# Attention, then two feed-forward layers, on one core: another order of the nine steps of a head pair

## The chip, the cores and the metric

The kernel runs on one core of a Trainium2 chip. The metric is the device time of one execution in microseconds (us); lower is better. Before the change it is 1013.62 us, the median of 3 runs (1011.56 to 1013.67).

## What is computed

Attention with a learned position bias, then two feed-forward layers over the 4 x 576 tokens, all in float32:

```python
scores = scale * q @ k.transpose(0, 1, 3, 2)      # (4, 8, 576, 64) each
bias = np.maximum((psi_rel / psi_i)[..., None] @ w1 + b1, 0.0) @ w2
scores = scores + bias.transpose(2, 0, 1)[None]
attn = np.exp(scores - scores.max(-1)); attn = attn / (attn.sum(-1) + 1e-9)
x = attn @ v                                      # to (2304, 512)
h = x @ w_in                                      # (2304, 1024)
solu = h * softmax(h); ln = (solu - mean) / sqrt(var + 1e-6) * g_ln
x = ln @ w_out
g = clipped square of x @ moe2_w_in               # (2304, 2048)
return g @ moe2_w_out
```

## The kernel before, in words

The program has four stages: the bias tables; attention; the first feed-forward layer, pipelined over tiles of 128 tokens; the second one. Each operand of a score or feed-forward product is held as a rounded part and a remainder (kh and kl for k, both in one tile sq for q, wih and wil for the weights), so that products of the rounded type keep the accuracy. Making these pairs is work for VectorE (the cast) and GpSimd (the subtraction).

Attention is one loop over k (L586), 144 steps of scores and eight more to empty the pipeline. Sixteen units u (a pair of heads hp and a batch b) have nine steps n each: two heads times four tiles of 128 queries, and a ninth step that takes the last 64 queries of both heads. The instructions go to each engine's queue in the order in which the program emits them, and an engine takes its queue in order. That order is written out by hand: `order[n]` (L582) is a string of letters for step n, and each letter emits one piece of work:

- Q, `emit_qk` (L381): four score matmuls (eight in step 8; L394) into one of two score buffers ps_s in PSUM, then the eviction L400 on VectorE, which adds the bias tile bt and keeps the smallest of each row. A score buffer is free again when its eviction is done. In the last batch of a head pair, Q also issues the bias loads of the next pair on the SP queue (L202).
- E, `emit_exp` (L411): the exponential of that step on ScalarE (L415); it needs the eviction of its step.
- T, `emit_T` (L446): on TensorE the transposes (L457, four of them, and L464, L465 or L471 in some steps) of the exponentials of five steps before, into one of three buffers ps_t, and copies to pt: ScalarE (L458, L466, L472), and in step 4 two small ones on VectorE (L467, L468).
- P, `emit_pv` (L474): the products with v, seven steps behind. It emits something in steps 1, 5 and 6 alone: called PV0, PV1 and PV2 here (L486, L490). PV1 ends in a copy by ScalarE (L496), PV2 in one by VectorE (L498). PV0 and PV1 share the only buffer ps_x; PV2 takes one of ps_t.
- r, R, M, S, N, `emit_norm` (L422), for the unit before: r the reciprocals of the row sums (L426, L427, VectorE), R their transposes to a ps_t buffer (L433, TensorE), M the product of output and reciprocals (L435, VectorE), S one transpose more (L438, TensorE), N the last two products (L443, VectorE).
- B, one step of `prep_all` (L172) for the next unit's q and k. Four steps make one of the two heads: the cast kh (L181, VectorE); the subtraction kl (L183, GpSimd) and the cast sq (L184, VectorE); the subtraction into the lower half of sq (L186, GpSimd) with the next load of q and k on the SP queue (L162); nothing. Eight steps of B a unit make both heads, kh0 to sq0 and kh1 to sq1 in the texts below. B starts in unit 1 and has nothing left in unit 15.
- W, one step of `split_w` (L273), which decodes a piece of the float64 weights of the first feed-forward layer into the pair. Four phases make one piece: (1) the subtraction of the piece before (L281, GpSimd) and three integer and float operations on VectorE (L291, L294, L295); (2) a ScalarE operation (L299); (3) one VectorE operation (L301), a product on GpSimd (L304) and the load of the piece after next on the SP queue (L323, L327); (4) a scaling (L309, for half of the pieces) and a cast (L310), both on ScalarE. There are 32 pieces; W acts from k = 6 on. Nine W a unit and four phases a piece: the phases that fall to a place in the unit move on by one from unit to unit, and come round after four.

After the loop's 144 steps `tail` (L585) gives the letters of the last steps, and what is left of W is emitted at once (L591).

Of the kernel before, what the change touches and what calls it, by code (L numbers as in the profile page):

```python
# [35 lines left out]
def tile_attention_moe_moe(  # L36
# [504 lines left out]
    def emit_post(i):  # L541
# [38 lines left out]


    order = [  # L582
        "PQTWBE", "QBrWTPEW", "QTBWPBE", "QTPEBW", "QBPTEW", "QPTWRE", "QPBMWTSBE", "PQTNE", "QTPWE",
    ]
    tail = {1: "TPr", 5: "TPR", 6: "TPMS", 7: "TPN"}  # L585
    for k in range(NK + LP + 1):  # L586
# [356 lines left out]
```

## Time and profile before

| what | value |
|---|---|
| median of 3 runs | 1013.62 us |
| the profiled execution: its own time | 1013.55 us |
| the profiled execution: span, first to last instruction | 1011.8 us |
| granted TensorE clock, mean | 0.997 |
| TensorE busy | 971.6 us (96%) |
| VectorE busy | 654.8 us (65%) |
| ScalarE busy | 549.1 us (54%) |
| GpSimd busy | 310.6 us (31%) |

How to read it: these are shares of the whole span, and the four stages have different limits; the change acts only on the attention loop, whose units 1 to 14 lie between 85.6 and 355.0 us. PE is TensorE, DVE VectorE, ACT ScalarE and POOL GpSimd. A matmul's end is modelled and matmuls overlap, so TensorE's busy time also holds part of what it loses; the starts of its groups tell more. In the rows, "idle before <- releaser" is the idle time of the engine just ahead of the instruction and what ended it.

### The profile page before, as it was taken

How to read it: one execution, taken by the hardware profiler on the slowest of the kernel's cores; microseconds unless marked ns; L12 is line 12 of the kernel's file. 1: busy time of each engine (PE TensorE's matmuls, PEld its weight loads, DVE VectorE, ACT ScalarE, POOL GpSimd, SP SyncE). 2: the span in 40 equal slices, each digit the busy share in tenths (PEclk: the TensorE clock that was granted, in tenths of full speed). 3: DMA queues.
4: the chain of work that ended last, by engine and by line, in shares of the span. 5: the costliest groups of instructions: out<-in, count | busy, mean ns of one | idle time of the engine just before them, and what ended most of it. 6: DMA issues, size and time to landing. Idle time of an engine off the chain costs nothing.

```text
span 1011.8 us, 16200 instructions
## 1 busy us (share of the span) xinstructions
PE 971.6 (96%) x6112; PEld 801.4 (79%) x6112; DVE 654.8 (65%) x1232; ACT 549.1 (54%) x1116; POOL 310.6 (31%) x277
## 2 busy tenths in 40 slices
PE   9998998998998999999999999989999999999998
PEld 6447777777786787898988898768888888888897
DVE  6878898898888844777777755775434433343343
ACT  6887777777788775656566643343222223222232
POOL 3313455455455412344556442340010011000000
PEclk9999999999999999999999999999999999999999
DMA  6994363363364200024454458710100100000010
GB/s 190 286 298 141 135 207 118 136 205 121 126 203 129 67 22 22 33 84 146 147 177 157 147 200 306 270 66 1 63 22 1 62 11 11 21 32 11 1 42 21
DMA packets 50046, 112.21 MB, mean 111 GB/s; under 512 B 7600, under 2 KB 13872, under 8 KB 49968
## 3 DMA queue, kind: packets, MB, share of 16 engines
q1 hardware_dynamic: 42688, 101.72, 30.3%
q0 software_dynamic: 2384, 4.74, 1.8%
q10 hardware_dynamic: 4896, 4.72, 1.4%
q8 instruction: 48, 0.79, 0.3%
q14 instruction: 30, 0.25, 0.1%
HBM read 80.34 MB, written 30.82 MB: 110 GB/s over the span
## 4 chain that ended last, share of the span: by engine, by line
PE 39%; issue 7%; POOL 6%; DVE 5%; ACT 2%; DMA 1%; ACTq 0%; POOLq 0%; DVEq 0%
PE acc L844 17%; PE h L820 16%; PE ps_x L696 3%; PE ps_s L535 2%; POOL wp L304 2%; POOL wdl L281 2%; DVE ga L827 1%; POOL xl L519 1%; DVE wp L291 1%; DVE raw L294 1%; POOL stb L568 1%; DVE ga L828 1%; PE ps_s L696 1%; DVE wp L295 1%; DVE stb L570 1%
## 5 line engine op out<-in xcount | busy, mean ns | idle before, releaser
L827 DVE SCALAR_TENSOR_TENSOR ga<-ga 128x512 f32<-128x512 f32 (+1 forms) x80 | 56.8, 710 | 157.3 <-ACT ga L826 157.3
L400 DVE CUSTOM_DVE_ANT_0 e<-ps_s,bt 128x576 f32<-128x576 f32 x144 | 107.5, 754 | 34.6 <-PE ps_s L394 30.0
L826 ACT ACTIVATE ga<-h,half_c 128x512 f32<-128x512 f32 (+1 forms) x80 | 51.6, 645 | 130.9 <-PE h L820 130.9
L304 POOL TENSOR_TENSOR wp<-raw,wp 128x256 f32<-128x256 f32 (+1 forms) x64 | 67.3, 1051 | 176.0 <-DVE wp L301 149.0
L394 PE MATMUL ps_s<-kh,sq 128*128 128x288 f32 x320 | 103.4, 340 | 18.6 <-DVE su L400 18.6
L415 ACT ACTIVATE e<-e,su 128x576 f32<-128x576 f32 x144 | 112.9, 784 | 13.5 <-DVE su L400 13.5
L820 PE MATMUL h<-x2h,w2l 128*128 128x512 f32 (+1 forms) x320 | 117.7, 368 | 0.0
L820 PE MATMUL h<-x2l,w2h 128*128 128x512 f32 (+1 forms) x320 | 117.7, 368 | 0.0
L820 PE MATMUL h<-x2h,w2h 128*128 128x512 f32 (+1 forms) x320 | 117.6, 368 | 0.0
L844 PE MATMUL acc<-w2h,gh 128*128 128x512 f32 x288 | 112.7, 391 | 2.5 <-ACT gh L829 2.5
L844 PE MATMUL acc<-w2h,gl 128*128 128x512 f32 x288 | 112.5, 391 | 1.5 <-DVE gl L831 1.5
L844 PE MATMUL acc<-w2l,gh 128*128 128x512 f32 x288 | 112.3, 390 | 0.0
L829 ACT CAST gh<-ga 128x512 fp32r<-128x512 f32 (+1 forms) x80 | 46.4, 581 | 120.6 <-DVE ga L828 120.6
L733 POOL TENSOR_TENSOR x2l<-x2f,x2h 128x512 fp32r<-128x512 f32 (+1 forms) x20 | 25.7, 1287 | 253.5 <-ACT x2h L732 253.5
L458 ACT COPY pt<-ps_t 128x512 f32<-128x512 f32 x144 | 83.5, 580 | 21.5 <-PE ps_t L457 19.4
L394 PE MATMUL ps_s<-kl,sq 128*128 128x288 f32 x320 | 89.7, 296 | 0.0
L457 PE MATMUL ps_t<-ident,e 128*128 128x128 f32 x576 | 86.4, 273 | 1.0 <-ACT pt L458 0.9
L831 DVE TENSOR_TENSOR gl<-ga,gh 128x512 fp32r<-128x512 f32 (+1 forms) x80 | 52.2, 653 | 48.5 <-ACT gh L829 48.3
L394 PEld LDWEIGHTS ps_s<-kh,sq 128*128 128x128 f32 x320 | 61.4, 192 | 23.8 <-DVE su L400 22.0
L696 PE MATMUL ps_x<-lh,woh 128*128 128x256 f32 x256 | 74.2, 290 | 5.6 <-ACT os L701 5.6
L696 PE MATMUL ps_x<-ll,woh 128*128 128x256 f32 x256 | 72.7, 284 | 0.4 <-DVE ll L685 0.4
L457 PEld LDWEIGHTS ps_t<-ident,e 128*128 128x128 f32 x576 | 70.4, 142 | 3.4 <-ACT pt L458 1.6
(147 smaller groups left out, 2332.0 us busy)
## 6 DMA issues: line engine op xcount, KB each, us to landing
stg<-in_qk_dram SPq DMA_DIRECT2D x30, 640.0 KB, 4.2
raw<-in_w2nd_dram SPq DMA_DIRECT2D x32, 512.0 KB, 3.7
bias_d<-ow SPq DMA_DIRECT2D x36, 295.5 KB, 4.6
w_d<-wdh SPq DMA_DIRECT2D x20, 256.0 KB, 2.8
w_d<-wdl SPq DMA_DIRECT2D x20, 256.0 KB, 2.5
w2h<-w_d SPq DMA_DIRECT2D x10, 512.0 KB, 5.3
w2l<-w_d SPq DMA_DIRECT2D x10, 512.0 KB, 6.0
v<-in_vp_dram SPq DMA_DIRECT2D x15, 320.0 KB, 3.0
```

The costliest lines, as they stand in the source:

```text
L304: nc.gpsimd.tensor_tensor(out=p, in0=t, in1=p, op=ALU.mult)
L394: nc.tensor.matmul(sc[:, hf, 0:HS], lhsT=l, rhs=r, start=j == 0, stop=j == len(parts) - 1)
L400: nc.vector.tensor_tensor_reduce(out=halves(e), in0=sc[:, :, 0:HS], in1=halves(b_t[hp, n]), scale=-1.0 / float(D) ** 0.5, scalar=3.0e38, o ...
L415: nc.scalar.activation(out=e, in_=e, func=ACTF.Exp, scale=-1.0, bias=su[:, n:n + 1], accum_out=su[:, 9 + n:10 + n])
L457: nc.tensor.transpose(tp[:, kt * 128:(kt + 1) * 128], e[:, c0:c0 + 128], ident)
L458: nc.scalar.copy(out=pt[:, 4 * h:4 * h + 4, 128 * o:128 * o + 128], in_=tp.rearrange("p (a b) -> p a b", a=4))
L696: nc.tensor.matmul(ob[:, a * 256:(a + 1) * 256], lhsT=l, rhs=r[:, f, :], start=f == 0 and j == 0, stop=f == K1 - 1 and j == 2,)
L820: nc.tensor.matmul(hp_, lhsT=l, rhs=r[:, kk, 0:n], start=kk == 0 and q == 0, stop=kk == KD - 1 and q == 2)
L826: nc.scalar.activation(out=a, in_=hp_, func=ACTF.Relu, scale=0.5, bias=half_c)
L827: nc.vector.scalar_tensor_tensor(out=a, in0=a, scalar=1.0, in1=a, op0=ALU.min, op1=ALU.mult)
L831: nc.vector.tensor_tensor(out=gl[:, 0:n], in0=a, in1=gh[:, 0:n].bitcast(F32), op=ALU.subtract)
L844: nc.tensor.matmul(acc_t[j][q], lhsT=l, rhs=r, start=f == 0 and m == 0, stop=f == K2 - 1 and m == 2)
```

## The change

Only the letters of `order` change; `tail` and all functions stay. Each string is for one step, 0 to 8.

```diff
     order = [
-        "PQTWBE", "QBrWTPEW", "QTBWPBE", "QTPEBW", "QBPTEW", "QPTWRE", "QPBMWTSBE", "PQTNE", "QTPWE",
+        "WBPQTE", "QBWrBEPT", "QPWTE", "QWBTPEWB", "BQPTE", "QPTWBRE", "PMWQBTWSE", "PQTNWE", "QTEP",
     ]
```

In step 0, W and B come ahead of Q. In step 1, W and the second B follow the first, E comes ahead of T, and PV0 ahead of T. Step 2 keeps one W and no B. Step 3 has W and B (an empty one of the four) behind Q and ends with W and B. In step 4, B comes ahead of Q and W is gone. In step 5, a B stands behind W. In step 6, PV2, M and W come ahead of Q, and one B and one W behind it. Step 7 gains a W. Step 8 loses its W. The unit has eight B and nine W before and after; P in other steps than 1, 5 and 6 emits nothing.

## Rows read from the trace of the kernel before

**Rows 1.** Stretch: us; busy us (instructions) of PE, PEld, DVE, ACT, POOL; clock; DMA, GB/s.

```profile
85.62:354.98 269.36, 246.26 (x2018) 203.95 (x2017) 240.07 (x546) 212.43 (x528) 135.96 (x119) 0.99 0.44 141
238.12:259.09 20.97, 18.92 (x147) 15.51 (x146) 18.10 (x39) 15.89 (x40) 9.39 (x8) 0.92 0.34 114
```

**Rows 2.** Waits of TensorE, 75 to 372 us: total us, times, longest us.

```profile
PE ps_s L394 <- DVE su L400: 18.6, 14, 2.1
PE ps_t L438 <- DVE xb L435: 4.0, 15, 0.3
```

**Rows 3.** Timeline of TensorE, unit 6 and the next start: start us, duration us, instruction.

```profile
181.58 0.38 PE L394 MATMUL ps_s<-kh,sq 128*128 128x288 f32 x1
...
182.55 0.38 PE L394 MATMUL ps_s<-kh,sq 128*128 128x288 f32 x1
...
183.80 1.95 PE L486 MATMUL ps_x<-pt,v 128*64 128x256 f32 x16
...
186.03 0.48 PE L394 MATMUL ps_s<-kh,sq 128*128 128x288 f32 x1
...
187.10 0.38 PE L394 MATMUL ps_s<-kh,sq 128*128 128x288 f32 x1
...
189.43 0.40 PE L394 MATMUL ps_s<-kh,sq 128*128 128x288 f32 x1 [1.13 <-DVE su L400]
...
190.64 0.38 PE L394 MATMUL ps_s<-kh,sq 128*128 128x288 f32 x1
...
194.99 0.38 PE L394 MATMUL ps_s<-kh,sq 128*128 128x288 f32 x1
...
195.70 0.69 PE L486 MATMUL ps_t<-pt,v 128*64 128x64 f32 x16
...
196.59 0.61 PE L457 MATMUL ps_t<-ident,e 128*128 128x128 f32 x4
...
197.98 0.32 PE L438 MATMUL ps_t<-ident,su 128*128 128x128 f32 x1 [0.27 <-DVE xb L435]
...
199.03 0.38 PE L394 MATMUL ps_s<-kh,sq 128*128 128x288 f32 x1
...
200.63 0.38 PE L394 MATMUL ps_s<-kh,sq 128*128 128x288 f32 x1
```

**Rows 4.** Timeline of VectorE, unit 6, steps 1 to 5.

```profile
183.54 0.74 DVE L400 CUSTOM_DVE_ANT_0 e<-ps_s,bt 128x576 f32<-128x576 f32 x1
...
184.22 1.32 DVE L184 CAST sq<-stg 128x640 fp32r<-128x640 f32 x1
...
186.31 1.60 DVE L291 TENSOR_SCALAR wp<-raw 128x256 uint32<-128x256 uint32 x1
187.95 0.43 DVE L294 SCALAR_TENSOR_TENSOR raw<-raw,wp 128x256 f32<-128x256 uint32 x1
...
188.62 0.75 DVE L400 CUSTOM_DVE_ANT_0 e<-ps_s,bt 128x576 f32<-128x576 f32 x1
...
193.43 0.34 DVE L291 TENSOR_SCALAR wp<-raw 128x256 uint32<-128x256 uint32 x1
```

**Rows 5.** Timeline of GpSimd, unit 6, steps 1 and 2.

```profile
183.76 1.43 POOL L183 TENSOR_TENSOR kl<-stg,kh 128x576 fp32r<-128x576 f32 x1 [0.45 <-PE ps_t L457]
...
186.20 1.56 POOL L186 TENSOR_TENSOR sq<-stg,sq 64x640 fp32r<-64x640 f32 x1
```

**Rows 6.** Timeline of VectorE and GpSimd, unit 5, step 4.

```profile
172.60 0.53 DVE L184 CAST sq<-stg 128x640 fp32r<-128x640 f32 x1
172.74 1.81 POOL L183 TENSOR_TENSOR kl<-stg,kh 128x640 fp32r<-128x640 f32 x1
```

**Rows 7.** Groups by line, VectorE, 85 to 350 us: count | busy us, mean ns.

```profile
L184 DVE CAST sq<-stg 128x640 fp32r<-128x640 f32 x28 | 34.9, 1246 | 0.0
L291 DVE TENSOR_SCALAR wp<-raw 128x256 uint32<-128x256 uint32 x31 | 29.7, 957 | 0.1
```

**Rows 8.** DMA issues of the page: count, KB each, median us to landing.

```profile
stg<-in_qk_dram SPq DMA_DIRECT2D x30, 640.0 KB, 4.2
```

## The prediction

> **What bounds the kernel now.** Read first the stretch table over the fourteen units u = 1 to 14, the only ones in which all nine steps carry preparation or weight splitting: 269.36 us from the first score matmul of unit 1 to that of unit 15, so 19.24 us a unit, with VectorE busy for 17.1, TensorE for 17.6, ScalarE for 15.2 and GpSimd for 9.7 of them [rows 1]. No engine is full, so it is the waits that have to be found. The waits of TensorE's queue come next: over the attention loop 18.6 us go to score matmuls that wait for the eviction L400 to free a score buffer, 14 of them, and 4.0 to the small transpose L438 that waits for the product L435 [rows 2]. Then one unit in order of time shows where [rows 3]. Call Q0 to Q8 the score groups, PV0 to PV2 the three products. Q3 starts at 187.10, Q4 should follow after the 0.97 us that lie between Q0 and Q1, at 188.07, and comes at 189.43: 1.36 us lost. The last product ends its issue at 196.59, when the next transposes start; from there to L438 are 1.39 us, of which the transposes between fill about 0.63 (0.61 for the four, a step for the fifth): 0.76 lost. The unit took 200.63 - 181.58 = 19.05 us, and without these two losses 16.93. **That is TensorE's floor**; the mean unit stands 19.24 - 16.93 = 2.31 above it. In unit 9 the granted clock was 0.92 on average and the unit took 20.97 us [rows 1]; that part I take to stay.
>
> Why Q4 is late is read from VectorE's own order [rows 4]. Q4 needs the buffer that eviction 2 frees. Q2 is issued at 186.03, but eviction 2 starts at 188.62, since behind the 0.68 us eviction 1 (183.54 to 184.22) stand the cast of sq (1.32 us), the small r pair and three weight operations, the first of 1.60 us. The same cast took 0.53 in the unit before, when it began just ahead of GpSimd's kl [rows 6]; in this unit kl ran from 183.76 for 1.43 us, to 185.19, and the cast ended 0.35 after it; and the slow weight operation began 0.11 us behind GpSimd's sq subtraction, which took 1.56 us [rows 5]. So a VectorE operation on SBUF operands that starts while GpSimd works stands until GpSimd is through. Evictions, which read PSUM, do not: 0.74 us at 183.54, beside kl [rows 4]. Over the fourteen units sq averages 1.246 and the first weight operation 0.957 [rows 7]: against 0.53 and the 0.34 that the weight operation takes when free, at 193.43 [rows 4], (28 x 0.72 + 31 x 0.62) / 14 = 2.8 us of standing a unit in these two lines alone.
>
> The Trainium skill ("SBUF — State Buffer", section "SBUF: two separate sides") says that VectorE and GpSimd share one port pair under an exclusive lock, which whoever starts first holds for its whole instruction; the rows above agree. By that rule a cast waits only for what is left of the other's instruction, so placing it later removes the wait; were 1.246 instead a fixed price of the cast, the Q4 waits would stay and the sum below would end at 1004.3, the first rival.
>
> **The change, part by part.** The letters of each unit are a permutation: Q, T, E, the three acting P, r, R, M, S, N once per place as before, eight B and nine W. No instruction is added; each price is a wait. I replay a unit by hand with the offsets of [rows 3], losses taken out: Q0 0, Q1 0.97, PV0 1.7 (0.71 behind Q1, as PV2 behind Q6), Q2 4.45, Q3 5.52, Q4 6.49, Q5 7.70, then PV1, transposes and R until 12.05, now PV2 ahead of Q6 with its 0.89 (195.70 to 196.59), so Q6 12.94, S 14.28, Q8 15.33, next unit 16.93. An eviction can start about 0.8 after its Q (an estimate: the 0.97 of a Q with its transposes, less part of these) and occupies 0.68; a Q needs the eviction two before it.
>
> *B in steps 0 and 1.* kh0 moves ahead of eviction 0, so evictions 0 and 1 (2 x 0.68) stand between kh0 and sq0 while kl0 (1.43) runs: sq0 finds almost none of it left, against 1.32 now. Gain about 0.7 of VectorE time. PV0 keeps TensorE for 2.23 [rows 3] behind Q1, so the delay of evictions 0 and 1 by kh0 and W falls under it.
>
> *B in steps 3 to 5.* kh1 and sq1 now stand back to back, so sq1 starts in the moment kh1 ends, ahead of kl1, which still has a semaphore to see. The nearest row is the 0.53 case, where kl waited instead [rows 6]; the far end is the 1.32 case. I take 0.53. Both casts, and in one unit of four a whole weight group (0.34 + 0.43 + 0.24, the last from the gap ahead of eviction 2, and what it stands for GpSimd), now delay eviction 4, to a start of about 9.6 in the worst unit instead of 7.3. Cover: its buffer is next wanted by Q6 at 12.94, 3 us later. Step 2 loses both B, so eviction 2 is followed by one W only.
>
> *W.* Its four phases shift by one each unit, so I take all four alignments. With phase 1 (the three long VectorE operations) at the start of step 0: all buffers in time. One unit later: none late. Phase 1 in step 2: eviction 3 ends at 7.63, Q5 about 0.1 late; and again in step 6 ahead of Q6's eviction: PV2's copy and L435 end near 13.9, W at 14.9, eviction 6 at 15.6, Q8 0.4 to 0.5 late. Phase 1 in step 1: GpSimd's sq0 subtraction (1.56) gets in between its operations, eviction 2 ends at 6.95 to 7.0 and Q4 is about 0.65 late. Sum 0.05 + 0 + 0.65 + 0.7 over four units, 0.35 a unit.
>
> *P and M ahead of Q in step 6.* Q6's matmuls, about 0.7, now lie between the product and the transposes that need L435's buffer. L435 follows at once on VectorE, nothing ahead of it: the S loss of 0.76 goes to about 0.1. Behind the waiting L435 stand W and eviction 6, counted above.
>
> *T behind PV0, E ahead of T.* PV0 loses 0.6 of lead on ScalarE's copies of step 8; they end near 1.4 in the worst unit and PV0 wants them at 1.7. Covered by 0.3, no more; with the scale copies of the second half of the weights it may cost 0.3 in a few units.
>
> *DMAs.* The next q and k loads (SP queue) follow the sq subtractions, now in steps 1 and 5 instead of 2 and 6. They need 4.2 us [rows 8] and are read a unit later; SP's bias loads behind them are wanted nine steps on. GpSimd's queue passes sq0's subtraction ahead of step 2's W, counted above. Nothing late.
>
> Sum: 0.35 replayed, 0.1 for S, and 0.4 for what a replay in tenths does not see and for unit 9's clock: 0.85 over the floor instead of 2.31. 14 x 1.46 = 20.4 us less; the rest of the program keeps its instructions and its waits. The profiled execution took 1013.55 (span 1011.8), the median of the runs is 1013.62, the same: **993.5 us**.
>
> **Rivals.** *Only step 6 gains (0.21).* The standing on VectorE is moved, not removed: sq0 or phase 1 meets kl and the subtractions in other places, and Q4, Q5 or Q8 wait as long as Q4 does now. For it: GpSimd still runs the same 9.7 us a unit. Against: the replay keeps its two longest runs apart from the casts. Price: 14 x (0.76 - 0.1) = 9.2 less, 1004.3.
>
> *The floor is reached (0.06).* All buffer waits go: 14 x (2.31 - 0.2) = 29.5 less, 984.
>
> *No difference (0.06).* The waits go round: 1013.5.
>
> *Slower: ScalarE sets the pace (0.09).* It takes its work in order, 15.2 us a unit, and exp 4 now waits for eviction 4 behind W, kh1 and sq1. If kl1 wins against sq1 (0.9 more) and phase 1 stands 1.3 for a subtraction, eviction 4 ends near 12.5; ScalarE stands about 2.4 there, 0.9 in step 0 for eviction 0, 0.4 and 0.7 where its weight casts wait for GpSimd: 15.2 + 4.4 = 19.6 a unit, 14 x 0.35 = 5 more, 1018.5. It turns at 4.0 us of such standing a unit; my replay has about 2. That the change does not do what it says is excluded by the letters: equal counts, and every M behind its R, every B and W in its own order.
>
> **How the numbers follow.** The forecast's own mechanism has 0.58, with 987 to 1000 as its range (0.4 to 1.3 over the floor). The 8-in-10 range takes in the first rival and a little of both ends: 985 to 1007. A measurement of this kernel tells about 0.2%, 2 us, from no change. Faster: 0.58 + 0.21 + 0.06 = 0.85; within: 0.06; slower: 0.09.
>
> **What would show it.** Right: unit starts 17.5 to 18 apart; sq casts near 0.55 in most units; L394's wait for L400 at 5 to 8 us instead of 18.6, found at Q8 and Q4; L438's wait gone; VectorE's busy time a unit down by 2 us or more with the same instruction count. Wrong: sq still above 1.2 on average (the rule of the remainder misapplied); L486 or L457 waiting for ScalarE's copies (the last rival); eviction 6 late in every unit (step 6 costs what it gives).

## The result, and the profile after

The changed kernel takes 989.43 us, the median of 4 runs (988.0 to 990.01), beside 1013.64 us before: a ratio of 0.9745, 95% interval 0.9719 to 0.9771. Forecast were 993.5 in a range of 985 to 1007. The profiled execution took 988.0 (span 986.2), 25.6 less than that of before.

All of it comes from units 1 to 14. The stretch from the first score matmul of unit 1 to that of unit 15, same columns as [rows 1]:

```profile
85.87:329.61 243.74, 241.84 (x2019) 201.58 (x2017) 200.08 (x545) 211.56 (x526) 136.28 (x120) 1.00 0.49 156
```

269.36 - 243.74 = 25.6 us. About 1.6 us of it is not the change: in the trace of before, unit 9 ran at a granted clock of 0.92 and took 20.97 us; in the run further below that moves letters of step 1 alone and gains nothing, the clock stayed at 1.00, unit 9 took 19.39 us and the fourteen units 267.84. A unit takes 17.41 us instead of 19.24, VectorE is busy for 14.3 of them instead of 17.1 with as many instructions, and ScalarE and GpSimd do what they did. The waits of TensorE's queue and VectorE's two lines answer to [rows 2, 7]:

```profile
PE ps_s L394 <- DVE su L400: 3.5, 9, 1.3
```

```profile
L184 DVE CAST sq<-stg 128x640 fp32r<-128x640 f32 x28 | 21.8, 780 | 0.0
...
L291 DVE TENSOR_SCALAR wp<-raw 128x256 uint32<-128x256 uint32 x31 | 14.8, 479 | 0.1
```

L438's wait is gone from the list, the score matmuls' is down from 18.6 to 3.5 us. This list of the matmuls shows only a part of each wait ([rows 3] has 1.13 us beside 1.36 lost at Q4). In the list of TensorE's weight loads, one ahead of each matmul, L394's waits fall from 22.0 to 5.8 us and L438's from 6.8 to nothing: 23.0 us, about the whole gain. VectorE's timeline in unit 6, whose Q0 starts at 172.59, shows how; it is the unit with phase 1 of W in steps 0, 3 and 7:

```profile
175.05 0.75 DVE L400 CUSTOM_DVE_ANT_0 e<-ps_s,bt 128x576 f32<-128x576 f32 x1
...
175.73 0.63 DVE L184 CAST sq<-stg 128x640 fp32r<-128x640 f32 x1
...
177.95 0.76 DVE L400 CUSTOM_DVE_ANT_0 e<-ps_s,bt 128x576 f32<-128x576 f32 x1 [1.26 <-PE ps_s L394]
...
179.65 0.45 DVE L291 TENSOR_SCALAR wp<-raw 128x256 uint32<-128x256 uint32 x1
180.13 0.43 DVE L294 SCALAR_TENSOR_TENSOR raw<-raw,wp 128x256 f32<-128x256 uint32 x1
180.59 0.78 DVE L295 TENSOR_SCALAR wp<-raw 128x256 uint32<-128x256 uint32 x1
181.28 0.48 DVE L181 CAST kh<-stg 128x640 fp32r<-128x640 f32 x1
181.68 0.48 DVE L184 CAST sq<-stg 128x640 fp32r<-128x640 f32 x1
182.08 0.75 DVE L400 CUSTOM_DVE_ANT_0 e<-ps_s,bt 128x576 f32<-128x576 f32 x1
...
185.86 0.23 DVE L498 COPY xb<-ps_t 128x64 f32<-128x64 f32 x1 [1.87 <-PE ps_t L490]
```

Between evictions 1 and 2 there are now sq0 (0.63 where [rows 4] has 1.32) and the r pair, and then VectorE is idle for 1.26 us until Q2's scores are there. Three weight operations and both casts stand between evictions 3 and 4 instead, under PV1: eviction 4 starts at 182.08, 9.5 us into the unit, and TensorE does not wait for it. (In units 1, 5, 9 and 13 phase 1 falls to step 1, and Q4 is still 0.3 us late.) GpSimd's timeline beside it:

```profile
181.90 1.68 POOL L183 TENSOR_TENSOR kl<-stg,kh 128x640 fp32r<-128x640 f32 x1 [0.70 <-issue]
```

kl1 is ready while sq1 runs, and it is kl that stretches (1.68 us; 1.55 in unit 6 of before), not the cast. The starts of five units on TensorE's timeline:

```profile
155.28 0.38 PE L394 MATMUL ps_s<-kh,sq 128*128 128x288 f32 x1
...
172.59 0.38 PE L394 MATMUL ps_s<-kh,sq 128*128 128x288 f32 x1
...
189.54 0.38 PE L394 MATMUL ps_s<-kh,sq 128*128 128x288 f32 x1
...
191.03 0.37 PE L394 MATMUL ps_s<-kh,sq 128*128 128x288 f32 x1 [0.29 <-DVE su L400]
...
207.01 0.38 PE L394 MATMUL ps_s<-kh,sq 128*128 128x288 f32 x1
...
224.69 0.38 PE L394 MATMUL ps_s<-kh,sq 128*128 128x288 f32 x1
```

They are 17.31, 16.95, 17.47 and 17.68 us apart. The row at 191.03 is one of the waits that are left, the Q1 of unit 7. Of all fourteen units only 2 and 6 come to the floor of 16.93 (16.95 each). Units 10 and 14, with W's phases in the same places, take 17.50 and 17.45: there the scaling L309, which only the second half of the pieces has, stands ahead of a copy on ScalarE (249.43, 0.51 us, in unit 10), and PV1 waits for that copy. PEld is TensorE's weight load:

```profile
250.91 1.49 PEld L486 LDWEIGHTS ps_x<-pt,v 128*64 128x64 f32 x14 [0.31 <-ACT pt L458]
```

### The profile page after: what moved, and what is told of

It reads as the page before. It is cut to its first block, busy times and chain, and to the rows that moved or that the text cites. A ratio compares the mean times of both kernels' runs of the same rounds, so it can differ in the third digit from the quotient of the medians.

```text
span 986.2 us, 16218 instructions
## 1 busy us (share of the span) xinstructions
PE 966.6 (98%) x6112; PEld 798.4 (81%) x6112; DVE 616.2 (62%) x1232; ACT 548.6 (56%) x1116; POOL 311.4 (32%) x277
## 4 chain that ended last, share of the span: by engine, by line
PE 40%; issue 8%; POOL 6%; DVE 5%; ACT 2%; DMA 0%; POOLq 0%; ACTq 0%; DVEq 0%
PE acc L844 17%; PE h L820 17%; PE ps_x L696 3%; PE ps_s L535 2%; POOL wp L304 2%; POOL wdl L281 2%; DVE ga L827 1%; POOL xl L519 1%; DVE wp L291 1%; DVE raw L294 1%; POOL stb L568 1%; DVE ga L828 1%; PE ps_s L696 1%; DVE wp L295 1%; ACT gh L829 1%
## 5 line engine op out<-in xcount | busy, mean ns | idle before, releaser
L304 POOL TENSOR_TENSOR wp<-raw,wp 128x256 f32<-128x256 f32 (+1 forms) x64 | 68.3, 1067 | 148.1 <-DVE wp L301 115.3
L733 POOL TENSOR_TENSOR x2l<-x2f,x2h 128x512 fp32r<-128x512 f32 (+1 forms) x20 | 25.6, 1281 | 253.2 <-ACT x2h L732 253.2
L394 PE MATMUL ps_s<-kh,sq 128*128 128x288 f32 x320 | 101.3, 334 | 3.7 <-DVE su L400 3.5
L394 PE MATMUL ps_s<-kl,sq 128*128 128x288 f32 x320 | 89.0, 294 | 0.0
L696 PE MATMUL ps_x<-lh,wol 128*128 128x256 f32 x256 | 72.1, 281 | 0.0
```

What stands on the lines that cost most here:

```text
L304: nc.gpsimd.tensor_tensor(out=p, in0=t, in1=p, op=ALU.mult)
L394: nc.tensor.matmul(sc[:, hf, 0:HS], lhsT=l, rhs=r, start=j == 0, stop=j == len(parts) - 1)
L696: nc.tensor.matmul(ob[:, a * 256:(a + 1) * 256], lhsT=l, rhs=r[:, f, :], start=f == 0 and j == 0, stop=f == K1 - 1 and j == 2,)
```

## The experiments

The question was which of the moved parts bring the gain, and by what. The diffs show the strings of the steps that an edit changes, in the order of the steps. Ratios are to the kernel before.

### One part alone, in the old order

Step 6 with PV2 and M ahead of Q:

```diff
-"QPBMWTSBE"
+"PBMQWTSBE"
```

> The kernel before, with only step 6 reordered: PV2 and M ahead of Q (its one B with them), W where it was. Theory A (two separate gains: casts moved out of GpSimd's way for the score waits, step 6 for the S wait): L438's wait of 4.0 us goes, the score waits on L400 stay near 18 us, the time falls by 14 x 0.66 = 9 us to about 1004. Rival B (step 6 is most of the gain, since Q6's matmuls fill the hole that also delays the rest): 995 or less. Rival C (step 6 gives with one hand and takes with the other, eviction 6 being later): 1011 to 1015, with a new wait of Q8.

Measured: 1008.94 us, ratio 0.9947 (0.9929 to 0.9965). TensorE's waits:

```profile
PE ps_s L394 <- DVE su L400: 19.3, 14, 2.1
PE ps_t L486 <- DVE pt L468: 1.4, 3, 0.6
...
PE ps_t L438 <- DVE xb L435: 0.4, 2, 0.2
```

Theory A by mechanism: L438's wait goes, the score waits stay. By size it is 0.53%, 5.4 us, not 9. (The trace is of an execution of 1012.97 us, 4 us above the median, with a granted clock of 0.92 in units 1 and 8.) A part of the rest shows: in some units PV2, now earlier, waits for the small copy L468, which stands behind eviction 4.

B alone:

```diff
-"PQTWBE", "QBrWTPEW", "QTBWPBE", "QTPEBW", "QBPTEW", "QPTWRE", "QPBMWTSBE"
+"BPQTWE", "QBrWBTPEW", "QTWPE", "QBTPEWB", "BQPTEW", "QPTWBRE", "QPMWTSBE"
```

> The kernel before, with only the eight B of a unit where the change puts them (ahead of Q in steps 0 and 4, twice in step 1, none in step 2, one in step 5); W, P, M, T and E stay. Theory A: sq casts average 0.8 us or less instead of 1.246, the score waits on L400 fall from 18.6 to under 10 us, L438's wait stays at 4, the time falls by 8 to 12 us to 1002 to 1006. Rival D (the weight operations' places matter, not the casts'): casts shorter, but the waits of Q4 stay above 15 us because W still stands ahead of evictions, 1010 or more.

Measured: 1008.11 us, ratio 0.9934 (0.9915 to 0.9953). TensorE's waits, then VectorE's lines:

```profile
PE ps_s L394 <- DVE su L400: 17.0, 17, 1.8
PE ps_t L438 <- DVE xb L435: 4.0, 15, 0.3
```

```profile
L291 DVE TENSOR_SCALAR wp<-raw 128x256 uint32<-128x256 uint32 x31 | 24.8, 801 | 0.1
...
L184 DVE CAST sq<-stg 128x640 fp32r<-128x640 f32 x28 | 19.6, 699 | 0.0
```

The casts are short and the score waits are nearly all there still. Here theory A failed and rival D held by its mechanism, though the time is under the 1010 that it named: short casts do not bring the evictions in time as long as the weight operations stand ahead of them.

W alone:

```diff
-"PQTWBE", "QBrWTPEW", "QTBWPBE", "QTPEBW", "QBPTEW", "QPBMWTSBE", "PQTNE", "QTPWE"
+"WPQTBE", "QBWrTPE", "QWTBPBE", "QWTPEBW", "QBPTE", "WQPBMTWSBE", "PQTNWE", "QTPE"
```

> The kernel before, with only the nine W of a unit where the change puts them (ahead of Q in step 0, one instead of two in step 1, two in steps 6, one in 7, none in 4 and 8); B, P, M, T and E stay. Theory A: the phase-1 operations still meet the subtractions, L291 stays above 0.7 us on average, the score waits change by less than half, time 1004 to 1014. Rival D: score waits under 8 us and 1002 or less.

Measured: 1005.83 us, ratio 0.9901 (0.987 to 0.9931). TensorE's waits, then the cast:

```profile
PE ps_s L394 <- DVE su L400: 6.6, 11, 1.5
PE ps_t L471 <- DVE xb L498: 4.1, 4, 1.0
PE ps_t L438 <- DVE xb L435: 4.0, 15, 0.3
```

```profile
L184 DVE CAST sq<-stg 128x640 fp32r<-128x640 f32 x28 | 33.6, 1199 | 0.0
```

The opposite picture: the casts stand as before and the score waits fall by 12 us. Theory A's limit (less than half) was wrong, and rival D's time was not reached, since W ahead of PV2's copy costs 4.1 us of waits at L471, 1.3 before, as long as step 6 is the old one.

Step 1's E, P and T alone:

```diff
-"QBrWTPEW"
+"QBrWEPTW"
```

> The kernel before with step 1 alone in the new order of E, P and T (QBrWEPTW): the part of the change that no other run isolates. Theory: PV0 loses 0.6 us of lead on ScalarE's copies and nothing else moves; within 2 us of before. If PV0 ahead of the transposes gives VectorE time to catch up, or ScalarE its copies late: 4 us or more either way.

Measured: 1014.62 us, ratio 0.9996 (0.998 to 1.0011): nothing, as forecast.

The four alone add up to 0.53 + 0.66 + 0.99 + 0.04 = 2.2%, of 2.55% together. B's share is the least sure: in its trace, at a granted clock of 1.00, the fourteen units take 263.6 us, 4.2 less than the 267.8 of the run just above, where its ratio stands for 6.7.

### One part undone, in the new order

Step 6 with Q first; then B; then W:

```diff
-"PMWQBTWSE"
+"QPMWBTWSE"
```

> The changed kernel, with Q ahead of PV2, M and W in step 6 again (QPMWBTWSE). Step 6 alone took 5.4 us off the old kernel. Theory A (step 6 is a gain of its own): L438's wait of about 4 us comes back, the score waits stay near 3.5 us, 5 to 7 us slower than the changed kernel, about 995. Rival B (in the new order step 6's Q needs its eviction early, so Q first is as good): 990 or less.

Measured: 995.13 us, ratio 0.9795 (0.973 to 0.986). Theory A: L438's 4.0 us are back, whole, and nothing else is:

```profile
PE ps_t L438 <- DVE xb L435: 4.0, 15, 0.3
PE ps_s L394 <- DVE su L400: 3.0, 6, 1.2
```

```diff
-"WBPQTE", "QBWrBEPT", "QPWTE", "QWBTPEWB", "BQPTE", "QPTWBRE", "PMWQBTWSE"
+"WPQTBE", "QBWrEPT", "QPBWTBE", "QWTPEBW", "QBPTE", "QPTWRE", "PBMWQTWSBE"
```

> The changed kernel with the eight B of a unit back where the old one has them relative to Q and E; W, P, M, T and E as changed. B alone took 6.7 us off the old kernel. If the parts add up (theory F): sq casts average 1.2 us again, score waits 8 to 10 us, 996. If W's places are what keeps the evictions in time, and a standing cast is then covered by PV0 and PV1 (theory G): sq casts at 1.2 all the same, score waits under 6 us, 990 to 993.

Measured: 995.01 us, ratio 0.9793 (0.974 to 0.9845). Theory F, the parts add up, by the median and by the score waits; the interval alone would leave theory G's upper end open. TensorE's waits, then the cast:

```profile
PE ps_s L394 <- DVE su L400: 9.6, 16, 2.2
```

```profile
L184 DVE CAST sq<-stg 128x640 fp32r<-128x640 f32 x28 | 36.1, 1290 | 0.0
```

```diff
-"WBPQTE", "QBWrBEPT", "QWBTPEWB", "BQPTE", "PMWQBTWSE", "PQTNWE", "QTEP"
+"BPQTWE", "QBrWBEPTW", "QBTPEBW", "BQPTEW", "PMQBWTSE", "PQTNE", "QTWEP"
```

> The changed kernel with the nine W of a unit back where the old one has them; B, P, M, T and E as changed. W alone took 10 us off the old kernel. Theory G (W's places keep the evictions in time): score waits near 15 us again, found at Q4, 999 to 1002, although the sq casts stay at 0.7 to 0.8 us. Theory A as predicted (the casts' places do most): score waits under 8 us, 993 or less.

Measured: 1002.69 us, ratio 0.9863 (0.9811 to 0.9915). Theory G, with short casts, 0.7 us above the range that it gave:

```profile
PE ps_s L394 <- DVE su L400: 16.7, 17, 1.8
```

```profile
L291 DVE TENSOR_SCALAR wp<-raw 128x256 uint32<-128x256 uint32 x31 | 27.0, 870 | 0.1
...
L184 DVE CAST sq<-stg 128x640 fp32r<-128x640 f32 x28 | 17.4, 620 | 0.0
```

W's places are the largest part, both ways round. The intervals of the first two overlap that of the changed kernel; what makes them readable is the wait that returns, and the fourteen units in the traces: at a granted clock of 1.00 throughout they take 248.7, 250.3 and 258.8 us with step 6, B and W undone, beside 243.7, so 5.0, 6.5 and 15.1 us more.

### GpSimd's subtractions taken away

These two say whether standing for GpSimd is the cause at all, or only VectorE's queue. The same edit in the old and in the new order; the computation loses its remainder of k and of half of sq (the diff leaves out the unchanged lines between):

```diff
-kl = wq.tile([128, n], F32R, tag=f"kl{h}", name="kl", bufs=2)
-nc.gpsimd.tensor_tensor(out=kl, in0=ks, in1=kh.bitcast(F32), op=ALU.subtract)
-nc.gpsimd.tensor_tensor(
-    out=sq[64:128], in0=st[64:128, 0:QW], in1=sq[64:128].bitcast(F32), op=ALU.subtract
-)
-kh_t[s], kl_t[s], sq_t[s] = kh, kl, sq
+kh_t[s], kl_t[s], sq_t[s] = kh, kh, sq
```

> The kernel before without GpSimd's two subtractions of the q and k preparation: the remainder of k is left out and the rounded part is used in its place, the lower half of sq keeps the rounded values; every matmul and every VectorE operation stays. It measures what standing for GpSimd costs in the old order. Theory A: sq casts near 0.5 us, L291 under 0.5, the score waits on L400 under 5 us, L438's wait stays at 4, time 1013.6 - 16 = about 997. Rival E (VectorE is late by its own work and by the order of the queue, not by GpSimd): sq still well over 0.6 or the score waits above 12 us, 1008 or more.

Measured: 989.98 us, ratio 0.9772 (0.9714 to 0.983); one of the four runs took 1001.17, the others 988.47 to 990.51. Lines are shifted by the edit: L389 is the score matmul, L395 the eviction, L433 and L430 are L438 and L435, L182 is the cast, L286 the first weight operation. TensorE's waits, then VectorE's lines and the stretch of the fourteen units with the columns of [rows 1]:

```profile
PE ps_t L433 <- DVE xb L430: 4.0, 15, 0.3
PE ps_s L389 <- DVE su L395: 3.5, 6, 1.4
```

```profile
L182 DVE CAST sq<-stg 128x640 fp32r<-128x640 f32 x28 | 14.9, 531 | 0.0
...
L286 DVE TENSOR_SCALAR wp<-raw 128x256 uint32<-128x256 uint32 x31 | 11.9, 383 | 0.1
```

```profile
87.12:331.96 244.84, 240.37 (x2016) 202.73 (x2017) 190.88 (x546) 211.64 (x528) 48.12 (x63) 1.00 0.47 154
```

In the old order, with every VectorE instruction in its old place, the score waits fall from 18.6 to 3.5 us and the time by 23 us (theory A, and 7 us more than it gave). VectorE is busy for 190.9 us of the stretch instead of 240.1, with as many instructions. So the old order lost its time by standing for GpSimd: rival E is out. W keeps its old places here and they cost little, so they too cost what they cost through the subtractions.

> The changed kernel without GpSimd's two subtractions of the q and k preparation (the remainder of k left out, its rounded part used in its place; the lower half of sq keeps the rounded values). Without them the old order took 990 us, 23 less than with them. Theory A and G (the old order lost its time by standing for GpSimd; the new one hardly meets it): 984 to 987, 2 to 5 us below the changed kernel, score waits under 2 us. If the new order still lost as much to other places (rival E): 975 or less; if the subtractions cost it nothing at all: 988 to 990.

Measured: 987.12 us, ratio 0.9713 (0.9661 to 0.9764), beside 0.9745 with the subtractions. The time is 0.1 us above what theories A and G gave, 2.3 us lower at the medians, which the intervals do not tell from nothing. Their score waits under 2 us did not come: the sum stays (3.6 us). The late Q4 of units 1, 5, 9 and 13 goes (unit 5 takes 17.01 us instead of 17.31), the late Q1 and Q8 of others stay, so most of what is left in the new order is not these subtractions.

### Three orders beyond the change

The rows of after show VectorE idle for 1.87 us ahead of PV2's copy L498 in unit 6. Three kernels try to use that hole.

```diff
-"PMWQBTWSE"
+"WPMQBTWSE"
```

> The changed kernel with step 6's first W ahead of PV2 (WPMQBTWSE): VectorE stands idle there for PV2, so the phase-1 operations would fill the hole instead of delaying eviction 6. Theory G: the late Q8 of every fourth unit goes, score waits from 3.5 to about 2 us, ratio to before about 0.973 (the changed kernel has 0.9745). If eviction 6 is not what Q8 waits for: no difference, 0.9745.

Measured: 985.6 us (984.77 to 986.27), ratio 0.9709 (0.9692 to 0.9727), the fastest order tried. Theory G by the waits; the ratio is 0.002 better than it gave. TensorE's waits, then VectorE's timeline in unit 4, where phase 1 falls to that W:

```profile
PE ps_s L394 <- DVE su L400: 2.4, 4, 1.4
PE ps_t L438 <- DVE xb L435: 0.3, 1, 0.3
```

```profile
148.64 1.44 DVE L291 TENSOR_SCALAR wp<-raw 128x256 uint32<-128x256 uint32 x1
150.11 0.97 DVE L294 SCALAR_TENSOR_TENSOR raw<-raw,wp 128x256 f32<-128x256 uint32 x1
151.12 0.30 DVE L295 TENSOR_SCALAR wp<-raw 128x256 uint32<-128x256 uint32 x1
151.32 0.22 DVE L498 COPY xb<-ps_t 128x64 f32<-128x64 f32 x1
```

Here L291 and L294 stand for GpSimd (1.44 and 0.97 us; 0.29 and 0.43 in the same unit of the changed kernel). In units 8 and 12 only L291 does (1.42 each), PV2's copy comes in time, and the units take 17.22 and 17.19 us instead of 17.68 and 17.70: the standing costs nothing that shows, since VectorE had nothing else to do. In unit 4 the hole is too small for both: Q7 comes 0.45 us late, and the unit takes 17.53, still under 17.68. The interval still touches that of the changed kernel (0.9719 to 0.9727), though no run of the one reaches a run of the other; the two were measured on different occasions. In the traces the fourteen units take 242.1 us, 1.6 less than in the changed kernel, of the 3.8 between the medians.

```diff
-"QPTWBRE", "PMWQBTWSE", "PQTNWE"
+"QPTWBWRE", "WPMQBTWSE", "PQTNE"
```

> As the one with W ahead of PV2, and step 7's W moved into step 5 behind R's letter order (QPTWBWRE, PQTNE): the cheap steps 7, 8, 0 and 1 then hold one W only. Theory G: the late Q1 of every fourth unit (0.35 us, phase 1 in step 7 ahead of eviction 8) goes too, score waits about 1 us, ratio 0.971 to 0.972. Rival: two W in step 5 put a ScalarE phase behind another and the copies come late, TensorE waits for ScalarE instead: 0.975 or more.

Measured: 990.73 us, ratio 0.9759 (0.9738 to 0.9779): a miss. The late Q1 goes as forecast (units 3 and 7 take 16.95 us), but more is lost elsewhere. The rival's time held, not its mechanism, since TensorE does not wait for ScalarE's copies but for VectorE:

```profile
PE ps_t L438 <- DVE xb L435: 1.6, 6, 0.3
PE ps_s L394 <- DVE su L400: 1.6, 3, 1.1
PE ps_t L471 <- DVE xb L498: 0.7, 2, 0.4
```

VectorE's timeline in unit 2 (17.88 us) shows why. Phases 1 and 2 of a piece are now both in step 5, so step 6's W is phase 3 (L301), and it waits for phase 2 on ScalarE (L299), with L498 and L435 queued behind it:

```profile
114.43 1.71 DVE L294 SCALAR_TENSOR_TENSOR raw<-raw,wp 128x256 f32<-128x256 uint32 x1
...
117.05 0.42 DVE L301 SCALAR_TENSOR_TENSOR wp<-raw,wp 128x256 uint32<-128x256 uint32 x1 [0.58 <-ACT wp L299]
117.39 0.22 DVE L498 COPY xb<-ps_t 128x64 f32<-128x64 f32 x1
```

```diff
-"QWBTPEWB", "QPTWBRE", "PMWQBTWSE"
+"QWBTPEB", "QPTWBRWE", "WPMQBTWSE"
```

> As the one with W ahead of PV2, and step 3's second W moved into step 5 (QWBTPEB, QPTWBRWE): eviction 4 then has only the two casts ahead of it. Theory G: eviction 4's lateness was covered already (its buffer is wanted by Q6 only), so no gain over the one with W ahead of PV2, 0.972 to 0.974. If that lateness cost something through the exponential of step 4 on ScalarE: 0.971 or less.

Measured: 989.32 us, ratio 0.9747 (0.9727 to 0.9766): no gain over the changed kernel, and worse than W ahead of PV2 alone. An earlier eviction 4 gained nothing, as forecast; that a second W in step 5 is free did not hold: with it, Q7 comes 0.3 to 0.5 us later in units 2, 6, 8 and 12 than with W ahead of PV2 alone.

## Why the prediction was right, and where its steps were off

**The floor and the place of the loss: right.** Two units of fourteen run at 16.95 us beside the 16.93 reckoned, and the whole gain lies in the fourteen units. Of the signs named, L438's wait went and VectorE's busy time fell by 2.9 us a unit; the unit starts (17.5 to 18 apart) and L394's wait (5 to 8 us) came out lower than named, 17.41 and 3.5.

**The cause: right.** Without GpSimd's subtractions the old order loses 15 us of its score waits. What the rule of the remainder said of sq0 holds: 0.63 us in unit 6 once two evictions stand between it and kh0, and 0.49 to 0.64 in ten units of fourteen. In units 4, 8 and 12 it takes 1.06 or 1.07, as kl0 begins later there and still has 0.7 to run.

**Which VectorE work matters: weighed wrongly.** The prediction put about as much standing on the sq casts as on W's first operation, 1.4 us a unit each. The runs put about 0.5 to 0.7% on B and 1.0 to 1.2% on W (their differences in ratio, alone and undone). With short casts and old places of W the score waits are 17.0 and 16.7 us; with long casts and the new places 6.6 and 9.6. The replay had W's places in it, so its sum did not suffer; the experiments' first expectations, which gave most to the casts, did.

**kh1 and sq1 back to back: right in five units of fourteen**, where nothing else of GpSimd's is pending: 0.47 to 0.49 us. In the other nine sq1 took 1.02 to 1.04, as a weight operation (L304, in two units L281) was running on GpSimd when it began. The forecast of casts near 0.55 in most units did not hold: the mean is 0.780, since GpSimd's weight operations were left out of that price. Without the subtractions the nine still take 1.02 to 1.04.

**The replay's waits: right in sum, not in place.** It gave 0.35 us a unit (the delays named ahead of that sum make 0.29 to 0.31) and 0.1 for S; the mean unit stands 17.41 - 16.95 = 0.46 above those that lose nothing. That these agree is in part luck. Where phase 1 falls to step 2 (units 4, 8 and 12) 0.73 to 0.75 us are lost, at Q5 and Q8 as reckoned (0.65). Where it falls to step 1, the late Q4 came smaller, 0.34 to 0.36 instead of 0.7. The late Q1 of units 3, 7 and 11 (0.5 to 0.7) had not been seen: phase 1 in step 7 of the unit before delays eviction 8. Nor had the stall in PV1 of units 10 and 14 (0.5); the prediction looked for ScalarE's late copies at PV0.

**Step 6: mechanism right, term too large.** 0.76 us was read from one unit and taken for all. Alone the edit brings 0.53%, 5.4 us or 0.39 a unit. Most of the rest of the 0.76 was standing once more: in unit 6 of before, the fifth transpose L471 itself waits for PV2's copy, which stands behind late evictions.

```profile
197.39 0.33 PE L471 MATMUL ps_t<-ident,e 128*128 128x128 f32 x1 [0.19 <-DVE xb L498]
```

In the old order without the subtractions L438, there L433, starts 1.08 us behind the four transposes in unit 6, not 1.39, with its own wait unchanged:

```profile
205.32 0.61 PE L452 MATMUL ps_t<-ident,e 128*128 128x128 f32 x4
...
206.40 0.32 PE L433 MATMUL ps_t<-ident,su 128*128 128x128 f32 x1 [0.27 <-DVE xb L430]
```

**The reserve: the term that was mis-sized.** 0.4 us a unit were kept for what the replay does not see and for unit 9's lower clock. The mean unit is 17.41 instead of the 17.78 reckoned, 14 x 0.37 = 5.2 us, about the whole reserve: next to nothing of it was needed. The granted clock over the fourteen units was 1.00 in the run shown, where [rows 1] has 0.92 in unit 9. Nor does the lower clock belong to the old order: the run with letters of step 1 moved has 1.00 in unit 9. Why it fell in the one trace was not tried.

**The rivals.** ScalarE did not set the pace. TensorE's list of matmuls shows no wait for its copies; the weight loads show small ones, and the one in PV1 lengthens units 10 and 14 by 0.5 us. L486 waiting for ScalarE is the sign that this rival named; it came in these two units only. "Only step 6 gains" fell, as B and W have their own gains.

## What to carry to other kernels

Where two engines block each other, ask not how long an operation stands but what is queued behind it: standing ahead of the evictions cost some 15 us of listed waits here, and 1.42 us of it ahead of a wait that was coming anyway cost nothing that shows. Find the stretches in which the bottleneck engine is busy with work that needs no buffer back, and put the blocking operations there; keep them out of the stretches in which every step returns a buffer. Two neighbouring phases of one pipeline in the same stretch made a new wait here.

## What the hardware showed that was not expected

An operation already waiting on VectorE went ahead of GpSimd's next one: in five units of fourteen, unit 6 among them, kh1 and sq1 took some 0.48 us each in a row, and kl, ready after kh1, stretched to 1.68. And the standing reached far down: the addition on nine numbers ahead of the reciprocals, L426, took 0.69 us in the old order's unit 6 while GpSimd worked, and 0.16 in the new one's.
